# Two tiles side by side in 640 columns: theta and channel products of a linear-attention and mixing kernel

## The chip, the core and the metric

The kernel runs on one core of a Trainium2 chip. A core has five engines that work at the same time, each on its own list of instructions, in order: TensorE (PE: matrix products and transposes, results in PSUM), VectorE (DVE), ScalarE (ACT), GpSimd (POOL) and SyncE (SP, which here only issues transfers). They wait for each other by semaphores. Transfers between the main memory and the on-chip memory run on 16 DMA engines, which all issuing queues share. The metric is the device time of one execution in microseconds (us).

## The reference

Two stages follow each other. The first is a recurrent linear attention, for 4 batches and 8 heads of 40 columns over 768 steps, with one 40x40 state a head:

```
y_t   = r_t . state
Sa    = state . a_t
state = state * w_t - Sa x b_t + v_t x k_t
```

The heads side by side give x, of shape 4 x 768 x 320. The second stage mixes x:

```
theta = x @ w_theta                       (320 x 320)
y     = w_tok_r @ (x cos theta) + w_tok_i @ (x sin theta)   (768 x 768, over the steps of a batch)
u     = x + y
out   = u + max(u @ w_ch, 0)              (320 x 320)
```

## The kernel before, in words

The 768 steps of a batch are cut into 6 chunks of 128, so there are 24 tiles, numbered through the batches. Within a chunk the recurrence is turned into products of 128x128 blocks (scores with a triangular mask); from chunk to chunk of a batch only the state is handed on.

The order of all work is written out by hand in the text ORDER (line 19). An entry names a step, its tile, the engine that does it (A ScalarE, V VectorE, G GpSimd, S a DMA transpose from SP's queue) and, after the @, a PSUM bank: `EKBT:3A` is the copy of the transposed kb of tile 3 on ScalarE, `TRK:4@3` the transposition of kb of tile 4 into bank 3. A loop at the end of the kernel (line 800) issues the entries one by one, and each engine keeps that order. So an entry decides at once the engine's order, the PSUM bank and, for loads, the place in a DMA queue. PSUM has four single banks (sm0 to sm3) and two double ones (sc0, sc1). An entry that takes a bank again waits until its last reader is done.

The steps that matter below, with their lines:

- Loads: LDW, LDK, LDB, LDA, LDV, LDR (lines 301 to 331) bring w, k, b, a, v, r of a tile or of two, 160 or 320 KB each, from SP's queue; four of the first ones go from ScalarE's queue (`LDK:0A` and so on). LDC brings w_theta and w_ch, LDT 128 rows of a token weight; both are converted to 16 bits on the way and are issued by GpSimd (lines 721 and 740).
- The decays: LN, CSI, INVW, CSE, WI (lines 333 to 420). CSI and CSE are cumulative sums, made by products of 64 rows, two of them at a time in the two halves of TensorE's rows. CSE also makes the totals of a chunk, with products of 128 rows. Then KH (line 422) multiplies k and b by the inverse decays and AH (line 428) a by the decays.
- Transposes by TensorE (TRK, TRA, TRR, TRV, NUT, GD, XT, UT, WT) and their copies out of PSUM (EKBT, EAT, ERT, EVT, ENUT, EGD, EXT, EUT, EWT).
- Scores: PSI, PHI, LV, LU (line 534), eight products of 64 rows each, two side by side; EPSI, EPHI, ELV, ELU copy them out with the mask, on VectorE in one step, or on ScalarE with the mask made afterwards by GpSimd (MPSI, MPHI, MLV, MLU).
- The recurrence: X0, ENX, NU, ENU, GT, EGT, and the output of the attention: Y, EX (line 641), which writes x of the tile.
- The second stage: XT transposes x in three blocks of 128 columns (line 646), EXT copies them out, TH (line 664) multiplies the three with w_theta, ETH copies theta out, SIN makes cosine and sine, ZR multiplies them by x. YR (line 688) is one block of the token product: `YR:7.3` adds the block of chunk 3 of the batch to the rows of tile 7, so the last one of a tile needs z of the whole batch. EU makes u, UT and EUT transpose it, CH (line 707) multiplies with w_ch, EO makes the output, ST stores it.

x and u of a tile lie in 384 columns: 320 with data, 64 that are zero from the beginning. Columns 256 to 383 are the third block, and the third rows of w_theta and w_ch are 64 rows with data and 64 zero rows. So each theta and each channel product is three products of 128 rows and 320 columns.

Of the kernel before, what the change touches and what calls it, by code (L numbers as in the profile page):

```python
# [25 lines left out]
KH:3G LV:1@1 NU:1 EKBT:2A LU:0@0 ELV:1V LDW:4 TRA:2@0 ENU:1A LDV:3 ELU:0A NUT:1@3 AH:3G EAT:2V
GT:1@1 ENUT:1V PSI:2@1 TRK:3@0 EGD:0V EPSI:2V LDK:4 LDA:4 GI:1 EKBT:3A CV:2G TRA:3@3 LU:1@0
ELU:1A CR:2G PHI:2@1 EGT:1V X0:2@2 EAT:3V EPHI:2V MLU:0G ENX:2A LN:4A LDB:4 TRR:2@0 PSI:3@0
LDR:4 CV:3G PHI:3@1 MLU:1G Y:0@1 EPSI:3A MPSI:3G EPHI:3V NU:2 TRV:2@3 CSE:4@0 LDV:4 ENU:2A
ERT:2A EVT:2V GT:2@2 EX:0V WI:4A AH:4G CSI:4@1 INVW:4A Y:1@3 LDW:6 NUT:2@1 EGA:2V EGT:2V ERT:3A  # L30
ENUT:2V LV:2@0 LDA:5 TRV:3@2 EX:1V X0:3@1 ELV:2A KH:4G EVT:3V LU:2@1 ENX:3V ELU:2V LV:3@0
TRA:4@0 ELV:3A LDK:5 NU:3 TRK:4@3 LDB:5 GD:1@2 EAT:4V ENU:3A MLV:2G XT:0@0 EKBT:4V CR:4A GT:3@1
GI:3 EGD:1V EGT:3V PSI:4@1 EPSI:4V CV:4G PHI:4@0 LN:6A TRR:4@3 EPHI:4A NUT:3@2 MLV:3G Y:2@1
ENUT:3V LDB:6 LDA:6 AH:5G LDK:6 CSI:6@1 X0:4@2 EX:2V EXT:0A ERT:4A INVW:6A TRV:4@0 ENX:4V
MPHI:4G LDV:5 KH:5G LU:3@0 ERT:5A XT:1@1 NU:4 ELU:3V EXT:1A CSE:6@1 LDV:6 LDT:1.1G ENU:4A
TRA:5@3 WI:6A NUT:4@1 EVT:4V ENUT:4A TRK:5@2 LDK:7 EAT:5V AH:6G XT:2@0 EKBT:5V LV:4@0 TH:0@3
ELV:4V KH:6G PSI:5@1 GD:2@1 LDR:6 SIN:0A TH:1@2 LU:4@0 CV:5G GT:4@3 GI:4 EXT:2A EPSI:5V CV:6G
ZR:0G LDW:8 TRA:6@0 PHI:5@1 LDB:7 ELU:4A LDA:7 EGD:2V EGT:4V TH:2@1 SIN:1A EAT:6V MLU:4G SIN:2A
TRK:6@3 X0:5@0 GD:3@2 EPHI:5V EKBT:6V ENX:5A LDB:8 Y:3@1 ZR:1G EGD:3V EX:3V PSI:6@0 EPSI:6V
TRV:5@3 TRV:6@2 Y:4@1 LN:8A LDK:8 NU:5 PHI:6@1 EVT:6V ENU:5V EVT:5A CR:6G X0:6@2 EPHI:6V  # L40
LDT:1.0G KH:7G TRR:6@0 ENX:6A CSI:8@0 INVW:8A LDA:8 LDV:7 EX:4V NUT:5@3 LV:5@1 ELV:5A LDB:9
ERT:6V AH:7G ENUT:5V TRK:7@1 CSE:8@0 ERT:7V KH:8G TRA:7@3 WI:8A LDV:8 LV:6@1 EAT:7V EKBT:7V
ELV:6A LU:5@0 LDA:9 GD:4@0 NU:6 ELU:5V AH:8G PSI:7@1 TRK:8@3 LDK:9 ENU:6A EGD:4A CV:7A MLV:5G
PHI:7@0 EKBT:8A ZR:2G GT:6@1 NUT:6@2 EPSI:7V EPHI:7A EGT:6V TRV:7@0 TRA:8@3 ENUT:6V LDW:10
X0:7@1 EVT:7V LU:6@1 ENX:7V LV:7@0 LDR:8 ELU:6V Y:5@2 EX:5V EAT:8A XT:3@0 MPHI:7G AH:9G NU:7
EXT:3V XT:4@3 ELV:7A PSI:8@1 EXT:4A GD:6@2 KH:9G EPSI:8A EGD:6V TRA:9@0 LDV:9 PHI:8@0 TH:3@3
EPHI:8V ENU:7A XT:5@2 ETH:3A MLV:6G EAT:9V TRK:9@1 LN:10A LDA:10 LDK:10 NUT:7@3 EKBT:9V MPSI:8G
GT:7@0 GI:7 ENUT:7V PHI:9@1 EGT:7V LU:7@0 EXT:5V CV:8G TH:4@1 SIN:3A LDB:10 CR:8G LDB:11 TH:5@3
SIN:4A X0:8@0 LDK:11 EPHI:9V TRR:8@2 MLV:7G Y:6@1 ENX:8A ELU:7V LDW:12 CV:9A LDT:0.1G SIN:5A
EX:6V NU:8 ENU:8A ERT:8V LDT:2.1G LDV:10 ZR:5G CSE:10@1 WI:10A PSI:9@0 EPSI:9V Y:7@1 NUT:8@3  # L50
GT:8@0 GI:8 LDA:11 CSI:10@0 LDR:10 EX:7V WT:1.1@1 ENUT:8V INVW:10A EGT:8V EWT:1.1V TRV:8@3
ERT:9A LU:8@1 ELU:8V X0:9@0 EVT:8A WT:1.0@1 ENX:9A KH:10G TRV:9@2 LDV:11 LV:8@0 NU:9 EWT:1.0A
ELV:8V AH:10G WT:0.0@3 EWT:0.0V TRK:10@1 EVT:9A LV:9@1 ENU:9A EKBT:10A ELV:9V TRA:10@2 EAT:10A
LDK:12 WT:0.1@0 KH:11G ZR:3G WT:2.1@3 NUT:9@1 LN:12A ENUT:9V EWT:0.1V PHI:10@0 PSI:10@1 EPHI:10A
EPSI:10V LDT:2.0G TRK:11@2 GD:7@1 LDA:12 GT:9@0 EGD:7A CSE:12@0 CR:10G CV:10A EGA:9V EGT:9V
LU:9@1 EWT:2.1A LDB:12 Y:8@1 AH:11G EKBT:11V WI:12A MPHI:10G X0:10@0 LDW:14 ENX:10V TRR:10@3
TRV:10@2 ELU:9A LDV:12 CSI:12@0 INVW:12A ERT:10A LDC:0.2G EX:8V NU:10 YR:0.0@1 YR:0.1 LDK:13
ENU:10V EVT:10V ZR:4G YR:0.2 LDB:13 XT:6@0 EXT:6V YR:0.3 ERT:11A MLU:9G LV:10@1 WT:2.0@2 ELV:10A
YR:0.4 TRA:11@0 EWT:2.0V YR:0.5 EAT:11V AH:12G GD:8@3 GT:10@2 PHI:11@0 EGD:8A EU:0V EGA:10V
EPHI:11A CV:11G PSI:11@1 NUT:10@0 KH:12G LDR:12 EGT:10V EPSI:11V ENUT:10A TRV:11@1 TH:6@3 EXT:8S  # L60
Y:9@2 LDA:13 EVT:11A ETH:6A TRK:12@0 EX:9V LDT:5.1G LN:14A X0:11@1 MPHI:11G LDV:13 EKBT:12V
# [772 lines left out]
```

## Time and profile before

| what | before |
|---|---|
| median of 3 runs | 207.43 us (206.94 to 208.84) |
| the profiled execution, its own time | 206.92 us |
| its span, first to last instruction | 205.2 us |
| PE busy | 190.1 us, 93% |
| VectorE, ScalarE, GpSimd busy | 170.6, 154.3, 147.1 us |
| moved by DMA | 34.17 MB, mean 167 GB/s |

The profile is of one execution. Busy time is the time in which an engine has at least one instruction running; on PE, where products overlap, a busy engine isn't one at its peak, so the distance between starts is read as well. In the rows below a group stands as line, engine, operation, output<-inputs, form, count, and behind the bar its busy time, the mean ns of one and the idle time before it. A row of a timeline gives the start in us, the duration, engine, line, operation and count. A row of a table by stretch gives the stretch, its length, and for PE, PE's weight loads, VectorE, ScalarE and GpSimd the busy us and the count, then the granted clock (1.00 is full), the DMA share and GB/s.

### The profile page before, as it was taken

Reading aid. Unit: us, or ns where it says so; the run is one execution under the profiler, and the core shown is the slowest. Engines: PE = TensorE matmul, PEld = TensorE weight load, DVE = VectorE, ACT = ScalarE, POOL = GpSimd, SP = SyncE. Lnnn points to the kernel's source line nnn. Section 1 sums busy time; section 2 is a strip of 40 time slices with the busy share of each in tenths; the row PEclk is TensorE's granted clock in tenths of the full one; section 3 lists DMA queues with packets and bytes.
Section 4 is the critical chain, followed back from the end, with each engine's and each line's share of the span. In section 5 each row is a group of like instructions: output and inputs, shape, how many; then the busy total and the mean of one; then the engine's idle time right before and its main releaser. Section 6 shows DMA issues by size and latency. Waiting matters only on the chain.

```text
span 205.2 us, 7809 instructions
## 1 busy us (share of the span) xinstructions
PE 190.1 (93%) x3266; PEld 147.5 (72%) x3266; DVE 170.6 (83%) x334; ACT 154.3 (75%) x259; POOL 147.1 (72%) x157
## 2 busy tenths in 40 slices
PE   0389999999999999999999999999999999999992
PEld 0166777877777887887887877887877787777671
DVE  7256899999999997999799998989888797975653
ACT  2367799997989997999899788987898685822100
POOL 8225778899989699998966886993989785634000
PEclk9999999999999999999999999999999999999999
DMA  7999999998898999899489989987979996433342
GB/s 136 187 240 159 225 171 178 173 230 140 153 221 154 213 159 216 164 213 226 103 171 193 192 172 238 192 135 161 169 97 154 218 129 140 99 90 103 102 150 96
DMA packets 144802, 34.17 MB, mean 167 GB/s; under 512 B 139520, under 2 KB 144768, under 8 KB 144768
## 3 DMA queue, kind: packets, MB, share of 16 engines
q1 hardware_dynamic: 138176, 30.26, 76.5%
q0 software_dynamic: 2432, 2.77, 8.4%
q10 hardware_dynamic: 4160, 0.66, 2.2%
q8 instruction: 25, 0.41, 0.9%
q14 instruction: 9, 0.07, 0.1%
HBM read 29.13 MB, written 3.93 MB: 161 GB/s over the span
## 4 chain that ended last, share of the span: by engine, by line
PE 80%; ACT 6%; DVE 5%; issue 2%; ACTq 2%; POOL 2%; POOLq 0%; DVEq 0%
PE sm L278 39%; PE sc L278 22%; PE sm L282 20%; ACTq L331 1%; ACT kbT L270 1%; ACT psi L270 1%; DVE phi L275 1%; ACTq L326 1%; ACT Wi_two L412 1%; ACT lw_two L338 1%; POOL z L275 1%; DVE lamu L275 1%; DVE rvT L272 1%; POOL lamv L554 1%; POOL phi L554 1%
## 5 line engine op out<-in xcount | busy, mean ns | idle before, releaser
L275 POOL TENSOR_TENSOR kb<-raw_kb,invW_two 128x640 bf16<-128x640 f32 x22 | 33.9, 1542 | 5.5 <-ACT invW_two L373 3.6
L275 POOL TENSOR_TENSOR z<-cs,x 128x640 bf16<-128x640 f32 x22 | 30.8, 1403 | 5.3 <-ACT cs L677 5.3
L278 PE MATMUL sm<-z,wtok_r 128*128 128x320 bf16 x120 | 34.3, 299 | 0.0
L278 PE MATMUL sm<-z,wtok_i 128*128 128x320 bf16 x120 | 34.2, 299 | 0.0
L275 POOL TENSOR_TENSOR ah<-raw_a,Wi_two 128x320 bf16<-128x320 f32 x22 | 19.0, 866 | 8.5 <-issue 5.2
L275 DVE TENSOR_TENSOR psi<-sc,mask_p 128x1024 bf16<-128x1024 f32 x16 | 19.5, 1219 | 1.0 <-PE sc L278 0.9
L554 POOL TENSOR_SCALAR_AFFINE_SELECT psi<-psi 128x1024 bf16<-128x1024 bf16 x8 | 8.7, 1093 | 14.0 <-ACT psi L270 11.6
L275 DVE TENSOR_TENSOR phi<-sc,mask_p 128x1024 bf16<-128x1024 f32 x14 | 17.1, 1219 | 1.6 <-PE sc L278 1.4
L278 PE MATMUL sc<-aT,kbT 64*128 64x128 bf16 x384 | 17.3, 225 | 1.1 <-ACT kbT L270 0.7
L275 DVE TENSOR_TENSOR lamu<-sc,mask_p 128x1024 bf16<-128x1024 f32 x14 | 17.1, 1220 | 0.6 <-PE sc L278 0.3
L282 PE MATMUL sm<-ident,kb 128*128 128x128 bf16 x184 | 14.9, 227 | 2.6 <-DVE kb L275 2.3
L278 PEld LDWEIGHTS <-wtok_r 128*128 128x128 bf16 x144 | 14.0, 97 | 4.6 <-issue 0.3
L270 ACT COPY rvT<-sm 128x512 bf16<-128x512 bf16 x28 | 15.9, 593 | 1.3 <-PE sm L282 0.7
L278 PEld LDWEIGHTS <-wtok_i 128*128 128x128 bf16 x144 | 14.1, 98 | 3.9 <-issue 0.2
L275 DVE TENSOR_TENSOR lamv<-sc,mask_p 128x1024 bf16<-128x1024 f32 x13 | 15.9, 1220 | 1.0 <-PE sc L278 0.5
L677 ACT ACTIVATE cs<-sm 128x320 f32<-128x320 f32 x26 | 9.9, 452 | 8.5 <-PE sm L278 8.4
L278 PEld LDWEIGHTS <-kbT 64*128 64x128 bf16 x384 | 11.9, 97 | 5.8 <-issue 2.4
L278 PEld LDWEIGHTS <-rvT 64*128 64x128 bf16 (+1 forms) x272 | 13.6, 95 | 2.9 <-issue 0.5
L278 PE MATMUL sm<-kb,lamv 128*128 128x40 bf16 x192 | 15.0, 180 | 0.0
L278 PE MATMUL sm<-kb,lamu 128*128 128x40 bf16 x192 | 14.9, 179 | 0.0
L282 PEld LDWEIGHTS <-kb 128*128 128x128 bf16 x184 | 11.5, 101 | 4.2 <-DVE kb L275 2.3
L554 POOL TENSOR_SCALAR_AFFINE_SELECT lamu<-lamu 128x1024 bf16<-128x1024 bf16 x10 | 10.9, 1090 | 4.1 <-ACT lamu L270 4.1
(137 smaller groups left out, 625.0 us busy)
## 6 DMA issues: line engine op xcount, KB each, us to landing
raw_w_two<-in_w_dram SPq DMA_DIRECT2D x12, 320.0 KB, 4.8
...
```

The lines of the kernel that those rows point to most:

```text
L270: keep(nc.scalar.copy(out=out, in_=in_))
L272: keep(eng[e].tensor_copy(out=out, in_=in_))
L275: keep(eng[e].tensor_tensor(out=out, in0=in0, in1=in1, op=ALU.mult))
L278: keep(nc.tensor.matmul(out, lhsT=lhsT, rhs=rhs, start=start, stop=stop, skip_group_check=True))
L282: keep(nc.tensor.transpose(out=out, in_=in_, identity=ident))
L326: keep(queue[e].dma_start(out=tiles[i].raw_kb[:, j], in_=source(ap, i)))
L331: keep(queue[e].dma_start(out=t, in_=source(ap, i)))
L338: keep(nc.scalar.activation(out=q.lw[:, :, :, 0:D], in_=q.raw_w.rearrange("p h (j d) -> p j h d", j=2), func=AF.Ln))
L412: keep(nc.scalar.activation(out=two, in_=q.cse[:, LO:LO + 2 * DM + 16], func=AF.Exp))
L554: keep(nc.gpsimd.affine_select(out=flat, in_=flat, compare_op=ALU.is_ge, fill=0.0, base=-1, pattern=[[0, 2 * G], [1, 128]], channel_multip ...
L677: keep(nc.scalar.activation(out=cs[i % 5][:, c], in_=tiles[i].theta, func=AF.Sin, bias=(math.pi / 2, 0.0)[c]))
```

## The change

Three things change together.

First, x and u of two tiles that follow each other lie in 640 adjoining columns, for u in all pairs, for x in the pairs from (6, 7) on. These are five blocks of 128 columns: the even tile is transposed in two blocks (its columns 0 to 255), the odd one in three (columns 256 to 639 of the pair, of which the first block holds the last 64 columns of the even tile and the first 64 of the odd one). Theta and channel products of the even tile are two products of 128 rows, those of the odd tile also two, and the mixed block serves both: two products of 64 rows, one in the upper and one in the lower half of TensorE's rows, into two PSUM banks (new entries THR and CHR, which stand under the odd tile's number). So the even tile's result is complete only after THR or CHR. The weights are held in five blocks, and LDC has eight entries instead of four.

Second, the totals of CSE are an entry of their own, CST.

Third, the whole of ORDER is written anew. Among much else all loads of inputs come from SP's queue, the entries of ScalarE's queue are gone, and eight loads of weights (`LDT:1.0 LDC:0.1 LDC:0.3 LDC:0.2 LDC:0.4 LDT:1.1 LDC:0.0 LDT:0.0`) stand ahead of GpSimd's other work, where three (`LDC:0.0 LDT:0.0 LDC:0.1`) stood. theta is buffered for three tiles instead of four.

The begin of ORDER in both, and what stands around the last output:

```
-LDW:0 LDK:0A LDB:0 LDA:0A LDA:1 LDB:1A LDK:1 LDV:0A LN:0A LDC:0.0G LDT:0.0G CSI:0@0 LDC:0.1G CSE:0@1 WI:0A
-INVW:0A KH:0V TRK:0@0 AH:0V EKBT:0A TRA:0@3 LDW:2 EAT:0V LDR:0 KH:1V PHI:0@1 PSI:0@0
-EPSI:0A MPSI:0G CV:0A LDB:2 EPHI:0A AH:1V TRK:1@1 EKBT:1V LN:2A TRA:1@2 MPHI:0G LDV:1 TRV:0@3
...
+LDT:1.0G LDW:0 LDC:0.1G LDK:0 LDC:0.3G LDB:0 LDA:0 LN:0A CSI:0@0 LDW:2 LDC:0.2G LDC:0.4G LDV:0
+CSE:0@1 INVW:0A LDT:1.1G LDC:0.0G CST:0 WI:0A LDT:0.0G LDK:1 KH:0V TRK:0@0 EKBT:0A AH:0V TRA:0@3
+LDB:1 LN:2A LDA:1 EAT:0V CV:0A PSI:0@0 PHI:0@1 LDR:0 EPSI:0V X0:0@1 LDV:1 CSE:2@0 EPHI:0V KH:1V
...
-XT:7@2 EXT:7A LDB:14 LDT:3.1G ENX:11V TRA:12@3 LU:10@0 LV:11@1 ELU:10V NU:11 GD:9@0 EAT:12A
-MLV:10G YR:1.0@2 ELV:11A LDA:14 TH:7@3 ENU:11V PSI:12@0 ETH:7A EGD:9V PHI:12@1 LDT:3.0G EPSI:12V
...
+LDT:4.1G EXT:6V EAT:12V GT:10@3 GI:10 TH:6@0 ELV:11A EGT:10V MLU:10G THR:7@2 PSI:12@1 EPSI:12V
+X0:11@1 CV:12G TH:7 ETH:6A AH:13G ENX:11A GD:9@3 LDW:16 YR:1.0@0 EGD:9A PHI:12@0 ETH:7V LN:14A
...
-YR:23.3 YR:23.4 YR:23.5 EU:22V UT:22@1 CH:21@0 EU:23V EUT:22A EO:21V UT:23@3 CH:22@2 EUT:23V
-CH:23@1 EO:22V ST:21 EO:23V ST:22 ST:23
...
+YR:23.3 EU:21V UT:21@0 ST:19 YR:23.4 YR:23.5 EUT:21V CH:20@1 CHR:21@3 EU:23V UT:22@0 UT:23@2
+EO:20V CH:21 EUT:22A EUT:23V ST:20 EO:21V CH:22@1 ST:21 CHR:23@0 CH:23 EO:22V EO:23V ST:22 ST:23
```

The functions:

```
+    x_two = [consts.tile([128, 768 if 2 * n < lone else 2 * DM], BF16, name=f"x_two_{n}")
+             for n in range(NCH)]
...
+    def home(i, twins, one, two):
+        if i not in twins:
+            t = one[i % len(one)]
+            return t[:, 0:DM], t
+        t = two[i // 2 % len(two)]
+        if i % 2:
+            return t[:, DM:2 * DM], t[:, 256:2 * DM]
+        return t[:, 0:DM], t[:, 0:256]
...
     def tr_three(i, b, name, src):
         pt = bank(b, BF16)
         setattr(tiles[i], name, pt)
-        for kt in range(3):
+        for kt in range(src.shape[1] // 128):
             transpose(pt[:, kt * 128:kt * 128 + 128], src[:, kt * 128:kt * 128 + 128])
...
+    def mix(i, b, name, lhs, rhs, twins):
+        q = tiles[i]
+        if i not in twins:
+            setattr(q, name, bank(b))
+            for kt in range(3):
+                mm(getattr(q, name)[:, 0:DM], lhs[:, kt, :], rhs[:, kt, :], kt == 0, kt == 2)
+        elif i % 2 == 0:
+            setattr(q, name, bank(b))
+            for kt in range(2):
+                mm(getattr(q, name)[:, 0:DM], lhs[:, kt, :], rhs[:, kt, :], kt == 0, False)
+        else:
+            for kt in range(2):
+                mm(getattr(q, name)[:, 0:DM], lhs[:, 1 + kt, :], rhs[:, 3 + kt, :], False, kt == 1)
+
+    def mix_ends(i, b, name, lhs, rhs):
+        setattr(tiles[i], name, bank(b))
+        for c in range(2):
+            mm(getattr(tiles[i - 1 + c], name)[:, 0:DM], lhs[rows(c), 0, :], rhs[rows(c), 2, :],
+               c == 1, c == 0)
...
     def weight_load(n):
-        dst, src = ((wth, moe_w_theta), (wch, moe_w_ch))[n // 2]
-        if n % 2 == 0:
-            keep(nc.gpsimd.dma_start(out=dst[:, 0:2, :], in_=src[0:256, :].rearrange(
-                "(a p) d -> p a d", p=128)))
+        dst, src = ((wth, moe_w_theta), (wch, moe_w_ch))[n // 4]
+        first, part = n % 2, n % 4 // 2
+        if part == 0:
+            keep(nc.gpsimd.dma_start(
+                out=dst[:, 3 * first:3 * first + 2, :],
+                in_=src[64 * first:64 * first + 256, :].rearrange("(a p) d -> p a d", p=128)))
         else:
-            keep(nc.gpsimd.dma_start(out=dst[0:64, 2, :], in_=src[256:320, :]))
+            keep(nc.gpsimd.dma_start(out=dst[rows(first), 2, :],
+                                     in_=src[256 * (1 - first):256 * (1 - first) + 64, :]))
```

More of the change, by code (lines that the diff above doesn't have):

```diff
@@ L26 @@
[L26 to L61, printed above, removed]
@@ new lines @@
+EXT:9S PSI:13@1 EX:11V EPSI:13A MPSI:13G EWT:3.1V CSE:14@0 CST:14 GT:12@0 EUT:0S WT:3.0@1
+EVT:13V UT:1@2 NUT:12@3 EGT:12V LN:16A WI:14A EUT:1V TRK:14@0 ENUT:12V EWT:3.0V LDT:5.1G
+WT:4.1@2 EKBT:14A AH:14G EWT:4.1V LDV:14 LU:12@1 ELU:12V LV:13@0 LDR:14 YR:3.0@3 ELV:13A AH:15G
+X0:13@1 LDK:15 YR:3.1 TRA:14@2 ENX:13A EAT:14V YR:3.2 YR:3.3 LDV:16 CH:0@0 CHR:1@2 MPHI:13G
+PHI:14@0 CV:14A EO:0V ST:0 PSI:14@1 CH:1 ZR:6G EPHI:14V NU:13 Y:12@0 ENU:13A YR:3.4 EPSI:14A
+EO:1V LDV:15 TH:8@1 YR:3.5 EX:12V MPSI:14G CR:14A THR:9@2 TH:9 ETH:9A EU:3V WT:5.1@0 TRV:14@3
@@ new lines @@
+ZR:10G ST:3 EKBT:17A TRA:17@0 LDW:20 EGA:15V YR:6.3 LV:16@1 ELV:16A CSE:18@0 EGT:15V MPHI:16G
+CST:18 WI:18A EAT:17V LDA:18 UT:5@2 X0:16@3 EUT:5V CH:4@0 ENX:16V CHR:5@2 EO:4V CSI:18@1 CV:17A
+PSI:17@0 NU:16 INVW:18A KH:18G CH:5 ST:4 YR:6.4 YR:6.5 EPSI:17V ENU:16A LDV:18 TRV:17@0 EVT:17A
+GD:14@3 EU:6V PHI:17@1 EGD:14V EO:5V NUT:16@1 LDB:19 XT:12@3 GT:16@0 ENUT:16V LDK:19 EPHI:17A
+EXT:12A EGA:16V EGT:16V Y:15@2 TRK:18@1 ST:5 TH:12@3 EXT:14S MPHI:17G EKBT:18V LV:17@0 THR:13@0
+AH:18G LU:16@1 EX:15V X0:17@1 ELU:16V CR:18G TH:13 TRA:18@2 LDW:22 SIN:12A ENX:17A YR:7.0@3
```

249 lines of the change are left out of this document (140 added, 109 removed).

## The prediction

> **What bounds the kernel now.** I read the page first, for the shares, then the table by stretch, for where each engine is full.
>
> ```profile
> span 205.2 us, 7809 instructions
> PE 190.1 (93%) x3266; PEld 147.5 (72%) x3266; DVE 170.6 (83%) x334; ACT 154.3 (75%) x259; POOL 147.1 (72%) x157
> PE 80%; ACT 6%; DVE 5%; issue 2%; ACTq 2%; POOL 2%; POOLq 0%; DVEq 0%
> ...
> 30.00:60.00 30.00, 29.39 (x613) 23.08 (x609) 28.71 (x51) 27.26 (x46) 27.75 (x28) 1.00 0.97 181
> 60.00:190.00 130.00, 129.51 (x2267) 101.94 (x2261) 114.41 (x200) 107.66 (x186) 103.14 (x102) 1.00 0.87 164
> 190.00:205.20 15.20, 11.54 (x89) 7.65 (x86) 7.78 (x17) 1.14 (x3) 0.00 (x0) 0.99 0.37 117
> ```
>
> The second number of a stretch is its length, then come PE, PE's weight loads, VectorE, ScalarE and GpSimd. From 60 to 190 us PE is busy 129.51 of 130 us, VectorE 114.41 (88%). Busy is not work, since matmuls overlap, so I look at starts: whether one matmul begins as soon as the one before allows.
>
> ```profile
> 102.13 0.30 PE L278 MATMUL sm<-z,wtok_i 128*128 128x320 bf16 x1
> 102.27 0.30 PE L278 MATMUL sm<-z,wtok_r 128*128 128x320 bf16 x1
> 102.40 0.30 PE L278 MATMUL sm<-z,wtok_i 128*128 128x320 bf16 x1
> 102.54 0.33 PE L282 MATMUL sm<-ident,x 128*128 128x128 bf16 x3
> 102.80 0.62 PE L278 MATMUL sc<-aT,kbT 64*128 64x128 bf16 x16
> 103.36 0.34 PE L282 MATMUL sm<-ident,nu 128*128 128x128 bf16 x3
> ```
>
> A 320-column product holds PE for 0.135 us (102.13, 102.27, 102.40). Three transposes take 0.26 us when 64-row products follow (102.54 to 102.80). There is no stall here beyond that, and the chain that ended last is 80% PE. So a microsecond of PE work removed after 60 us is a microsecond of time, if the new list keeps PE as full. Before 60 us the four engines are all at 91 to 98%, and before that the loads count.
>
> **The change part by part.**
>
> *Products of theta and channel (THR, CHR).*
>
> ```profile
> L278 PE MATMUL sm<-wch,uT 128*128 128x320 bf16 x72 | 13.7, 300 | 0.1
> L278 PE MATMUL sm<-wth,xT 128*128 128x320 bf16 x72 | 13.2, 299 | 0.0
> L282 PE MATMUL sm<-ident,x 128*128 128x128 bf16 x57 | 6.3, 220 | 0.1
> L282 PE MATMUL sm<-ident,u 128*128 128x128 bf16 x42 | 4.6, 219 | 0.1
> ```
>
> Three products a tile, 72 for theta and 72 for the channels; the third is half zeros. Nine pairs of x tiles (6 to 23) and all twelve pairs of u tiles go from six full products to four full and two of 64 rows. That takes away 42 x 0.135 = 5.7 us. What a pair of 64-row products costs shows where the kernel already makes such pairs, in the cumulative sums: four of 64x320, two and two side by side.
>
> ```profile
> 37.66 0.18 PE L278 MATMUL sm<-kb,lamv 128*128 128x40 bf16 x1
> 37.68 0.18 PE L278 MATMUL sm<-kb,lamu 128*128 128x40 bf16 x1
> 37.79 0.45 PE L278 MATMUL sc<-lw_two,pair_inc 64*128 64x320 bf16 x4
> 38.17 0.21 PE L278 MATMUL sm<-gt,aT 128*128 128x80 bf16 x1
> ```
>
> Four take 0.38 us to the next start (37.79 to 38.17). One after another they would need 4 x 0.135 = 0.54, so they do run side by side: two steps of 0.135 are 0.27, and 0.11 us is left, the price of going back to 128 rows. The way in costs about 0.09: a 128x40 product has 0.02 to the next (37.66 to 37.68), ahead of the 64-row ones 0.11 (37.68 to 37.79); likewise 0.26 against 3 x 0.056 for the transposes above. A visit to 64 rows thus costs 0.19 us beside its work. So: added 21 pairs x 0.135 = 2.8 us, net -2.8 us, plus or minus the visits.
>
> That last part could undo the change: 21 lonely pairs would cost 21 x 0.19 = 4.0 us. I counted the visits in both lists, taking neighbouring score, sum and pair products as one: 84 before, 81 after, because the totals of the cumulative sum became a step of their own (CST) and 13 of the 21 pairs stand beside other 64-row products (PSI, PHI, LV, LU, CSI or another pair). So -3 x 0.19 = -0.6 us. The Trainium skill, "TensorEngine Tiling (Array Packing)", Key Properties, says that changing the tiling mode drains TensorE; the trace agrees, with 0.09 us in and 0.11 us out. By that rule with no regard to neighbours this part would come out at +1.2 us instead of -3.4.
>
> *Transposes.* The even tile of a pair is transposed in two blocks instead of three, and more go by the DMA transpose. On PE the x transposes fall from 57 to 39, the u ones from 42 to 29; six more for the token weights and four each of NUT and TRV come in, four of GD go: net -21 x 0.056 = -1.2 us, all after 60 us but a few. DMA transposes rise from 28 to 34 on SP's queue. They stand behind other entries of that queue, and every load behind them waits; I take 0, between 0 and 6 x 1.2 us of SP (an x transpose holds SP 1.2 us by its row), which costs only where a load is late.
>
> ```profile
> L448 SPq DMA_TRANSPOSE xT<-x x5: 1184/1207/1672, 82.0 to 185.4; - x5
> ```
>
> *PE in all:* -2.8 - 0.6 - 1.2 = -4.6 us.
>
> *The other engines.* The new list moves work between them.
>
> ```profile
> L275 DVE TENSOR_TENSOR lamu<-sc,mask_p 128x1024 bf16<-128x1024 f32 x14 | 17.1, 1220 | 0.6 <-PE sc L278 0.3
> L272 DVE COPY rvT<-sm 128x512 bf16<-128x512 bf16 x18 | 8.8, 491 | 0.8 <-PE sm L282 0.7
> L523 DVE TENSOR_SCALAR nx<-sm 128x320 bf16<-128x320 f32 x13 | 6.4, 489 | 2.3 <-PE sm L278 2.0
> L272 DVE COPY kbT<-sm 128x1024 bf16<-128x1024 bf16 x16 | 11.0, 686 | 2.3 <-PE sm L282 2.2
> ```
>
> VectorE: two more masked scores (+2.4), eight more r and v copies (+3.9), eleven fewer nx and nu (-5.4), three fewer kbT (-2.1), and a net of six more small copies of about 0.42 (+2.5): +1.3 us on 170.6. ScalarE loses some 4 us, GpSimd is unchanged. Until tile 18 VectorE does about 6 us more than before and after that as much less. It has 12% to spare after 60 us, so I take 0, and keep +3 us as the far end, half of that bulge.
>
> *The start.* Two things oppose each other. For: the inverse weights (INVW) come ahead of WI, and the first scores are masked on VectorE in one step.
>
> ```profile
> 7.83 0.72 ACT L412 ACTIVATE Wi_two<-sc 128x656 f32<-128x656 f32 x1 [1.68 <-PE sc L278]
> 9.17 0.83 DVE L275 TENSOR_TENSOR kb<-raw_kb,invW_two 128x640 bf16<-128x640 f32 x1 [3.76 <-ACT invW_two L373]
> 14.36 1.08 POOL L554 TENSOR_SCALAR_AFFINE_SELECT psi<-psi 128x1024 bf16<-128x1024 bf16 x1 [8.13 <-ACT psi L270]
> 17.78 1.54 POOL L275 TENSOR_TENSOR kb<-raw_kb,invW_two 128x640 bf16<-128x640 f32 x1 [1.07 <-ACT invW_two L373]
> 22.45 1.54 POOL L275 TENSOR_TENSOR kb<-raw_kb,invW_two 128x640 bf16<-128x640 f32 x1
> ```
>
> That saves the 0.72 of Wi ahead of the first kb, about 0.5 of products, and the 1.08 of the GpSimd mask: 2.3 to 3.5 us on tile 0. Against: eight loads stand at the head of GpSimd's queue instead of three (192, 160, 40, 40, 160, 192, 160 and 192 KB, 1136 KB instead of 392), and the four early loads of ScalarE's queue (q10) move to SP's (q1). The three windows' DMA rows:
>
> ```profile
> q1 hardware_dynamic: 2525, 0.40, 73.6%
> q10 hardware_dynamic: 2357, 0.37, 70.9%
> ...
> q0 software_dynamic: 469, 0.39, 80.6%
> q1 hardware_dynamic: 704, 0.13, 32.2%
> q10 hardware_dynamic: 407, 0.07, 17.0%
> ```
>
> From 4 to 8 us (first two rows: packets, MB, share) the input loads move 0.77 MB, 0.19 a us. From 8 to 11 us GpSimd's 0.39 MB are moved and the inputs get 0.20 MB, 0.07 a us. With 1136 KB that stretch lasts 3 x 1136/392 = 8.7 us, and 5.7 us more at 0.07 instead of 0.19 is 0.7 MB, or 3.6 us of loading; if q10's turns fall away too, 0.04 a us, it is (0.19 - 0.04) x 8.7 less (0.19 - 0.07) x 3, 0.9 MB or 4.9 us. It strikes k and b of tiles 1 to 3: their kb steps, at 17.78 and 22.45 before, come some 4 us later, and tile 1 waits for data that tile 0's earlier finish can't use. By 30 us both stand near the first x tile, VectorE some 1.3 us behind. The Trainium skill, "DMA: Bandwidth & Descriptors", Queues, rings and completion order, has each DMA engine take turns between queues packet by packet; the fall from 0.19 to 0.07 agrees, and by it the inputs lose one of their two turns here. I take +2 us for the start; from -2 (only the gain counts) to +5 (all the delay).
>
> *The end.* The last row product starts at 199.35, the last output step at 201.69.
>
> ```profile
> 199.35 0.30 PE L278 MATMUL sm<-z,wtok_i 128*128 128x320 bf16 x1
> 201.69 0.49 DVE L715 SCALAR_TENSOR_TENSOR oo<-sm,u 128x320 f32<-128x320 f32 x1
> ```
>
> In the new list the outputs of 22 and 23 both wait for the last pair, so one 0.49 us step comes after instead of between; and theta of 22 is closed only with x of 23, so z of 23 follows later than the 2.7 us of PE work in the list covers: I take +0.7, between 0 and 1.5.
>
> *The sum.* -4.6 + 2 + 0.7 = -1.9 us. The profiled execution took 206.92 us (205.2 span and 1.7 around it): 205.0. It lies at the low end of the runs shown (median 207.43, 206.94 to 208.84), so for a median I add 0.2: **205.2 us**, 1.1% under the median. The bounds of the terms: -4.6 - 2 = -6.6 at best, and -4.6 + 5 + 1.5 + 3 = +4.9 at worst.
>
> **The rivals.**
>
> - *PE's saving comes through whole and the start gains* (no loss by the loads, since before 60 us something else binds): -4.6 - 0.5 to -1, 201.5 to 202.5. For it: tile 4 needs its k only late; the DMA waits in the trace of before are few. Against: by the turns above tile 1 must wait.
> - *The loads bind the start* (turns taken by GpSimd's eight loads): +4.9 instead of +2, and VectorE's bulge behind it, +1 to +3: 206.9 - 4.6 + 4.9 + 0.7 + 1 is 208.9, with +3 it is 210.9; half of it within 1%. It decides if kb of tile 2 starts after 23 us.
> - *Slower: the closing product waits.* A pair's even half can't be read before the odd tile's transposed copy lies in SBUF, the pair stands in PE's queue, and all behind it stands too; two banks are held meanwhile, of four. Price: the wait, 21 times. A copy of 0.35 to 0.5 us and its two hand-overs against the PE work that the list puts between (for 11, 3 and 5 it is 0.8 to 1.1 us, for 23 0.8) leaves little. From 0.1 us a pair the gain of 1.9 is gone; at 0.25 us a pair it is +5.3 - 1.9, 210.5 us. Against: the trace of before shows no waits of PE for copies after 60 us.
> - *The pairs don't run side by side* (banks or rows conflict): +21 x 0.135 = +2.8, 208 us. Against: the four 64x320 products in 0.38 us.
>
> **How the numbers follow.** Forecast 0.50 (203 to 207.4; two thirds of it over 1% faster), whole saving 0.13, loads 0.20, closing product 0.13, not side by side 0.04. The likeliest case's own range is 203 to 207.4. The range of all is 201.5 to 210.2: below it lies a little of the whole saving, above it the closing product's upper part and a third of the loads, together under 0.2. About 1%, 2 us, is what a measurement of this kernel tells from no change. Faster by over 1%: 0.33 + 0.13 = 0.46. Slower by over 1% (over 209.5): the closing product 0.13 and half of the loads 0.10, 0.23. The rest, 0.31, within 1%.
>
> **What would show it.** In the profile after: 64x320 products of wch and wth, 24 and 18 of them, two by two starting together; about 0.135 us to the next 64-row start; PE's rows 21 fewer; between 60 us and the end no PE wait over 0.3 us for xT or uT copies. For the start: q0's stretch from 8 us to 16 or 17, kb of tile 1 after 16 us and of tile 2 near 22. If kb of tile 2 stands at 18, the start term is wrong; if PE's waits behind 60 us sum to over 3 us, the sum is wrong at the premise that PE stays full.

## The result, and the profile after

| | before | after |
|---|---|---|
| median of 4 runs | 208.13 us (206.94 to 210.64) | 214.89 us (213.04 to 215.20) |
| ratio after to before | | 1.0329, 95% interval 1.0280 to 1.0378 |
| span of the profiled execution | 205.2 us | 213.5 us |

The changed kernel is 3.3% slower; 205.2 us and a range up to 210.2 us were forecast. Medians here are over all executions; the ratios leave out those that took over 1.5% longer than the kernel's fastest (two of four in e8 and e18 below, one of four in e4 and e12), so a ratio can differ from the quotient of two medians.

The page of the changed kernel, same parts as shown of before (span, busy time, the chain that ended last):

```profile
span 213.5 us, 7781 instructions
PE 189.1 (89%) x3245; PEld 143.5 (67%) x3245; DVE 172.3 (81%) x327; ACT 152.3 (71%) x252; POOL 147.6 (69%) x158
PE 45%; DMA 19%; DVE 11%; ACT 8%; POOL 8%; SPq 4%; issue 3%; DVEq 0%; POOLq 0%; ACTq 0%
```

PE's rows are 21 fewer, as foretold, but its share of the chain fell from 80 to 45%, and DMA, which was not in it, has 19%. The table by stretch of the changed kernel (columns as before: stretch, length, PE, its weight loads, VectorE, ScalarE, GpSimd, clock, DMA share, GB/s):

```profile
30.00:60.00 30.00, 28.48 (x589) 22.54 (x587) 27.87 (x48) 28.50 (x48) 25.73 (x26) 1.00 0.99 183
60.00:190.00 130.00, 126.22 (x2264) 97.72 (x2263) 114.02 (x201) 104.72 (x173) 103.39 (x103) 1.00 0.90 162
190.00:213.50 23.50, 17.60 (x144) 10.50 (x141) 11.50 (x24) 3.88 (x11) 3.67 (x3) 0.98 0.34 104
```

From 60 to 190 us PE is busy 126.22 us where it was 129.51, for almost the same number of instructions (2264, 2267). What it stood for is in the view of waits. Behind 60 us the kernel before has one row, the changed one ten (who waited, for whom: us in total, times, longest):

```profile
PE sm L282 <- ACT nu L521: 0.2, 1, 0.2
```

```profile
PE sm L296 <- DMA uT<-u_two: 1.2, 2, 0.7
PE sm L300 <- DMA wtok_row<-in_moe_w_tok_i_dram: 0.7, 1, 0.7
PE sm L296 <- POOL psi L575: 0.6, 1, 0.6
PE sm L300 <- POOL ah L293: 0.6, 2, 0.4
PE sc L296 <- DVE u_two L742: 0.6, 1, 0.6
PE sm L296 <- ACT nu L542: 0.6, 1, 0.6
PE sm L300 <- DVE rvT L290: 0.4, 1, 0.4
PE sm L300 <- ACT rvT L288: 0.4, 1, 0.4
PE sm L296 <- DMA xT<-x_two: 0.4, 1, 0.4
PE sc L296 <- DVE kbT L290: 0.2, 1, 0.2
```

They sum to 5.7 us, for DMA, VectorE, ScalarE and GpSimd in turn, none of them the one new bound. The prediction named a sum over 3 us as the sign that its premise is wrong, and any wait over 0.3 us for xT or uT as a sign against it: here they come to 0.7.

The view leaves out short waits. So I also measured from the starts of PE's instructions: for each two that follow each other, by group and form, the distance's lower quartile over all traces of this study is taken as work, and what a distance has beyond it (over 0.04 us) as standing. By stretch, in us; "first" is PE's first product, "last" the time from PE's last start to the end:

| kernel | first | work | standing | 0-60 | 60-160 | 160-end | last |
|---|---|---|---|---|---|---|---|
| before | 6.2 | 165.6 | 29.5 | 15.6 | 11.2 | 2.8 | 3.8 |
| after | 4.9 | 161.2 | 43.4 | 20.8 | 14.7 | 7.9 | 4.0 |

Work fell by 4.4 us (4.6 were priced), the first product comes 1.3 earlier, the last part is 0.2 longer, and PE stands 13.9 us more: +8.4 in all, against 8.3 between the spans. So the question of the experiments is where 13.9 us of standing come from. The 29.5 us of before hold the start and the short hand-overs that any list has. The measure is an estimate: other ways to pool the neighbours move all rows alike by up to 3 us, and against each other by about 1 us, e4 below by 2 and e7 by 4; the difference between before and after stays within 0.3.

### The profile page after: what moved, and what is told of

Read it like the earlier page. It is cut to its first block, busy times and chain, and to the rows that moved or that the text cites. A ratio compares the mean times of both kernels' runs of the same rounds, so it can differ in the third digit from the quotient of the medians.

```text
span 213.5 us, 7781 instructions
## 1 busy us (share of the span) xinstructions
PE 189.1 (89%) x3245; PEld 143.5 (67%) x3245; DVE 172.3 (81%) x327; ACT 152.3 (71%) x252; POOL 147.6 (69%) x158
## 4 chain that ended last, share of the span: by engine, by line
PE 45%; DMA 19%; DVE 11%; ACT 8%; POOL 8%; SPq 4%; issue 3%; DVEq 0%; POOLq 0%; ACTq 0%
PE sm L296 21%; PE sc L296 12%; PE sm L300 12%; DMA raw_kb<-in_b_dram 7%; DMA wtok_row<-in_moe_w_tok_i_dram 3%; DMA raw_v<-in_v_dram 3%; DMA raw_a<-in_a_dram 2%; POOL kb L293 2%; DVE rvT L290 2%; DMA uT<-u_two 2%; DVE lamu L293 2%; POOL ah L293 2%; ACT rvT L288 1%; POOL z L293 1%; ACT kbT L288 1%
## 5 line engine op out<-in xcount | busy, mean ns | idle before, releaser
L293 POOL TENSOR_TENSOR kb<-raw_kb,invW_two 128x640 bf16<-128x640 f32 x22 | 33.9, 1540 | 23.7 <-ACT rvT L288 13.5
L293 POOL TENSOR_TENSOR z<-cs,x_two 128x640 bf16<-128x640 f32 x22 | 30.7, 1402 | 4.5 <-ACT cs L714 4.5
L293 DVE TENSOR_TENSOR lamu<-sc,mask_p 128x1024 bf16<-128x1024 f32 x21 | 25.6, 1217 | 1.7 <-PE sc L296 1.7
L296 PE MATMUL sc<-aT,kbT 64*128 64x128 bf16 x384 | 18.3, 225 | 1.9 <-ACT kbT L288 0.7
L300 PE MATMUL sm<-ident,kb 128*128 128x128 bf16 x184 | 14.9, 228 | 5.6 <-DVE kb L293 4.9
L293 DVE TENSOR_TENSOR psi<-sc,mask_p 128x1024 bf16<-128x1024 f32 x14 | 17.1, 1220 | 3.0 <-PE sc L296 2.9
L288 ACT CAST lamv<-sc 128x1024 bf16<-128x1024 f32 x14 | 14.2, 1014 | 4.4 <-PE sc L296 4.4
L751 DVE SCALAR_TENSOR_TENSOR oo<-sm,u_two 128x320 f32<-128x320 f32 x24 | 11.6, 488 | 6.9 <-PE sm L296 6.8
L296 PEld LDWEIGHTS <-kbT 64*128 64x128 bf16 x384 | 12.5, 98 | 6.4 <-issue 2.3
L575 POOL TENSOR_SCALAR_AFFINE_SELECT psi<-psi 128x1024 bf16<-128x1024 bf16 x10 | 10.9, 1092 | 8.3 <-ACT psi L288 6.7
L290 DVE COPY rvT<-sm 128x512 bf16<-128x512 bf16 x26 | 14.3, 560 | 2.0 <-PE sm L300 1.1
L575 POOL TENSOR_SCALAR_AFFINE_SELECT lamv<-lamv 128x1024 bf16<-128x1024 bf16 x14 | 15.3, 1093 | 0.8 <-ACT lamv L288 0.8
L296 PE MATMUL sm<-kb,lamu 128*128 128x40 bf16 x192 | 14.9, 180 | 0.0
```

Of the source, the lines that this page charges most:

```text
L288: keep(nc.scalar.copy(out=out, in_=in_))
L290: keep(eng[e].tensor_copy(out=out, in_=in_))
L293: keep(eng[e].tensor_tensor(out=out, in0=in0, in1=in1, op=ALU.mult))
L296: keep(nc.tensor.matmul(out, lhsT=lhsT, rhs=rhs, start=start, stop=stop, skip_group_check=True))
L300: keep(nc.tensor.transpose(out=out, in_=in_, identity=ident))
L575: keep(nc.gpsimd.affine_select(out=flat, in_=flat, compare_op=ALU.is_ge, fill=0.0, base=-1, pattern=[[0, 2 * G], [1, 128]], channel_multip ...
```

## The experiments

All runs of three rounds; the ratio is to the kernel before on the same chip. Standing is by the same measure as above, in brackets where the profiled execution is one that the ratio leaves out, so that it reads too high. It also holds what PE loses where its clock is lowered (see e12).

| run | median us | ratio (95% interval) | PE work | standing | 0-60, 60-160, 160-end |
|---|---|---|---|---|---|
| after | 214.89 | 1.0329 (1.0280 to 1.0378) | 161.2 | 43.4 | 20.8, 14.7, 7.9 |
| e1 late weights | 212.58 | 1.0204 (1.0135 to 1.0274) | 161.3 | 40.2 | 19.0, 14.9, 6.4 |
| e2 before, eight loads | 210.46 | 1.0105 (1.0045 to 1.0165) | 165.4 | 33.9 | 18.3, 11.6, 3.9 |
| e3 unpaired | 213.71 | 1.0283 (1.0205 to 1.0361) | 162.7 | 39.6 | 20.7, 13.1, 5.8 |
| e4 tail on PE | 216.05 | 1.0366 (1.0280 to 1.0453) | 162.0 | 43.4 | 21.5, 14.2, 7.7 |
| e5 old start | 216.70 | 1.0466 (1.0402 to 1.0531) | 162.0 | 43.1 | 17.5, 18.4, 7.2 |
| e6 old start, unpaired | 217.50 | 1.0518 (1.0444 to 1.0592) | 164.5 | 41.3 | 16.5, 17.8, 7.0 |
| e7 pairs in old list | 237.35 | 1.1454 (1.1379 to 1.1529) | 165.8 | 61.1 | 17.8, 26.6, 16.7 |
| e8 late, unpaired | 212.12 | 1.0144 (1.0084 to 1.0204) | (162.8) | (40.3) | (18.1, 15.7, 6.5) |
| e9 loads ahead | 213.36 | 1.0306 (1.0225 to 1.0388) | 161.0 | 41.6 | 18.8, 18.3, 4.5 |
| e10 mid transposes on PE | 216.76 | 1.0506 (1.0421 to 1.0591) | 163.3 | 42.9 | 17.9, 18.0, 7.0 |
| e11 a on ScalarE's queue | 220.38 | 1.0619 (1.0501 to 1.0737) | 161.5 | 48.2 | 20.7, 21.0, 6.4 |
| e12 before, more DMA transposes | 225.42 | 1.0881 (1.0781 to 1.0982) | (165.0) | (50.4) | (15.8, 23.9, 10.7) |
| e13 new then old | 209.84 | 1.0109 (1.0070 to 1.0148) | 164.1 | 35.5 | 18.5, 13.6, 3.4 |
| e14 old then new | 214.11 | 1.0319 (1.0259 to 1.0380) | 164.6 | 36.8 | 16.5, 14.1, 6.1 |
| e15 new then old, late | 213.50 | 1.0274 (1.0221 to 1.0328) | 163.4 | 41.5 | 17.9, 19.7, 4.0 |
| e16 old then new, late | 220.17 | 1.0606 (1.0556 to 1.0656) | 165.1 | 44.2 | 16.9, 20.1, 7.2 |
| e17 three parts | 213.36 | 1.0302 (1.0273 to 1.0332) | 165.7 | 35.6 | 16.8, 14.5, 4.4 |
| e18 old start, paired, loads mended | 213.11 | 1.0205 (1.0129 to 1.0282) | (163.0) | (38.9) | (16.7, 15.6, 6.6) |

### The start: the early loads (e1, e2)

e1 delays four of the changed kernel's eight first loads:

```
-LDT:1.0G LDW:0 ... LDC:0.2G LDC:0.4G ... LDT:1.1G LDC:0.0G ... LDT:0.0G
+LDW:0 ... LDC:0.2G ... LDC:0.0G ... AH:4G LDT:0.0G ... AH:5G LDT:1.1G ... AH:6G LDT:1.0G ... LDC:0.4G LDC:0.5G
```

> The changed kernel with four of its eight early weight loads (three of a token weight, one of w_ch, 736 KB of 1136) moved to between 35 and 90 us. Theory (start): the eight loads take the DMA engines from the inputs of tiles 1 to 3, and the delay lasts to the end since every engine is full afterwards: kb of tile 1 back from 16.9 us to 12 or 13, of tile 2 from 22.8 to 18 or 19, and the time 4 to 5 us shorter, 210 to 211 us beside 214.9. Rival (later): the start's delay is taken up by slack behind it and the time is lost in waits after 50 us: kb comes earlier likewise, but the time falls by less than 1.5 us.

e2 gives the kernel before as many early loads:

```
-... LDC:0.1G ...
+... LDC:0.1G LDT:1.1G LDT:1.0G LDC:0.2G LDC:0.3G LDT:2.1G ...
```

> The kernel before, with five more weight loads at the head of GpSimd's queue (three of token weights, two of w_ch, so 1168 KB there instead of 392). Theory (start): inputs of tiles 1 to 3 come some 4 us later, and so does the end: 3 to 4.5 us longer than before. Rival (later): less than 1.5 us longer.

Delaying the four loads gains 1.25 points of ratio, 2.6 us; adding them to before costs 2.2 us (0.9 to 3.4). The rows of the changed kernel say how: from 7 to 15.5 us GpSimd's queue moves 1.16 MB and the inputs 0.51 (packets, MB, share of 16 engines), 0.06 MB a us.

```profile
q0 software_dynamic: 1402, 1.16, 83.5%
q1 hardware_dynamic: 3046, 0.51, 42.2%
```

In the chain of work of the changed kernel (start, us, what), b of tile 1 lands after 10.23 us; in e1 the same load takes 6.20:

```profile
6.62 10.23 DMA raw_kb<-in_b_dram
16.94 0.83 DVE kb L293
...
22.80 1.54 POOL kb L293
```

```profile
6.75 6.20 DMA raw_kb<-in_b_dram
```

So the loads cost about 2.4 us in time. But e1 was to come to 210 or 211, and its 212.58 is still 2% slower than before: the larger part lies elsewhere.

### The pairs (e3, e7, e8)

e3 is the changed kernel's list with whole products (THR and CHR taken out, three products a tile, u in five buffers):

```
-TH:6@0 ... THR:7@2 ... TH:7
+TH:6@0 ... TH:7@2
```

> The changed kernel in its own order but without pairs: every theta and channel product three full products again, THR and CHR gone, transposes of three blocks, u in five buffers. PE's work rises by 21 x 0.135 us of products and 7 x 0.056 us of transposes and falls by 7 visits to 64 rows of 0.19 us: +1.9 us. Theory (PE's saving is real): about 2 us longer than the changed kernel, 216 to 218 us. Rival (the closing product waits): the even tiles no longer wait for the odd ones, so it is as fast or faster, 212 to 215 us.

PE's work rises by 1.5 us and its standing falls by 3.8, of which 2.1 behind 160 us; the time is the same within the intervals, rather shorter. The 3.8 us read too high for the pairs: the profiled executions are the longest of the changed kernel and the shortest of e3, 2.2 us apart, where the medians are 1.2 apart. The waits for DMA uT, 1.2 us with pairs, are 0.2 without, those for the token row and for ScalarE's nu are gone (waits of PE behind 60 us in e3):

```profile
PE sc L290 <- DVE u L736: 0.6, 1, 0.6
...
PE sm L290 <- DMA uT<-u: 0.2, 1, 0.2
PE sc L290 <- DVE kbT L284: 0.2, 1, 0.2
PE sm L294 <- POOL ah L287: 0.2, 1, 0.2
```

e7 puts all 21 pairs into the list before. What follows an even tile's product (its copy, its output step) moves behind the pair with it, the totals CST are their own entry and LDC has eight; the rest keeps its order:

```
-TH:6@3 ... TH:7@3
+(at the odd tile's place) TH:6@a THR:7@b TH:7      likewise CH, CHR
```

> The list before with all 21 pairs, nothing else reordered: the even tile's product is moved to the odd one's place (with what follows it), the rows of the weights that the pairs need are loaded in two more loads behind 45 us. The list has 100 visits to 64-row mode instead of 84, since most pairs stand alone there. By the profile's prices: 21 pairs instead of 42 tail products -2.8, transposes -1.2, 16 visits at 0.19 +3.0, in sum -1.0: 207.2 us if nothing waits. If the closing pair waits for the odd tile's copy, and other work behind it in TensorE's order with it: over 209 us.

Not 1 us faster but 30 us slower. PE's work, 165.8 against 165.6, has changed little (the estimate is good to 4 us here); its busy time from 60 to 190 us fell from 129.51 to 112.86 (table by stretch of e7), and the waits of e7 behind 60 us are of another kind:

```profile
60.00:190.00 130.00, 112.86 (x1922) 83.94 (x1918) 96.86 (x166) 96.16 (x161) 92.75 (x95) 0.97 0.80 148
```

```profile
PE sm L298 <- DVE oo L749: 3.7, 7, 1.0
PE sm L298 <- ACT cs L712: 3.4, 4, 1.7
PE sc L294 <- ACT rvT L286: 2.2, 1, 2.2
PE sm L298 <- ACT kbT L286: 2.1, 1, 2.1
PE sm L294 <- ACT rvT L286: 1.3, 1, 1.3
PE sm L298 <- ACT th L286: 1.0, 2, 0.5
```

The closing product's own input is little of it: a row not shown has 0.6 us, in two waits, for the copy uT. The largest rows are oo and cs, with th 8.1 us: steps that read the results of pairs out of their banks, before the transposes (L298) that come next can have a bank. A pair holds two of the four single banks and hands both to the readers at one time, and this fits. But 8.1 us are not 30. The other rows wait for copies of operands, and three stretches of 3.4 us at half the granted clock (see e12) cost up to 5 us more in the profiled execution; what put those copies late was not followed up. So pairs put into a list as it stands lose far more than they save.

e8 takes both away, pairs and early loads. It leaves the new order and what came with it: inputs from SP's queue alone, eight loads of w_theta and w_ch, three buffers of theta:

> The changed kernel with the late start loads of the first experiment and without the pairs: the new order alone. Additive by the two single runs (-2.3 and -1.2): 211.4 us, which leaves 3.2 us to the new order itself against 208.2 before, although its list has 10 visits to 64-row mode fewer (1.9 us). If the two hide each other: 212.5 us.

Its ratio lies within 1.0084 to 1.0204, that of e1 (with pairs) within 1.0135 to 1.0274. Twice, then, taking the pairs out has changed nothing that these runs can tell. What is left, 1.4% or 3.0 us by the ratio and 2.1% by the medians of all (212.12, before 207.77), is the new order's with what came with it, although its PE work is 2.8 us less than before: transposes fewer, and its list has 74 visits to 64-row mode instead of 84.

### SP's queue and the DMA transposes (e4, e9 to e12)

The chain has 19% DMA, so I suspected SP's queue, on which loads stand behind waiting DMA transposes. e4 makes five late DMA transposes on PE; e9 moves the loads ahead; e10 makes twelve DMA transposes of the middle on PE; e11 lets ScalarE issue the loads of a; e12 gives the kernel before eight of the DMA transposes that the changed one has and it has not.

```
e4:  -EUT:14S EUT:15S EUT:16S EUT:17S EXT:22S   +UT:14@2 EUT:14A ... XT:22@1 EXT:22A
e9:  every LDK, LDB, LDA, LDV, LDR, LDW 30 entries earlier, or right behind what frees its buffer
e10: -EXT:8S ... EUT:11S                        +XT:8@0 EXT:8A ... UT:11@3 EUT:11V
e11: -LDA:6 ... LDA:23                          +LDA:6A ... LDA:23A
e12: -XT:9@0 EXT:9V ... UT:4@3 EUT:4A           +EXT:9S ... EUT:4S
```

> The changed kernel with the last DMA transposes (u of 14 to 17, x of 22) made by TensorE and copied by ScalarE, which is idle for two thirds of that time. In the trace PE stands 0.9, 0.5 and 0.6 us for those transposes between 192 and 198 us; the five transposes add 0.7 us to PE. Theory (late transposes at the end): 1.5 to 2 us shorter, near 213 us. Rival (another step is late in their place): within 0.5 us of 214.9.

> The changed kernel with the late start loads (212.6 us), and behind tile 2 every input load that SP issues stands 30 entries earlier in the list, or right behind the step that frees its buffer (21 entries earlier on average), so ahead of the waiting DMA transposes of x and u. Theory S (SP's queue is the bound of the new order: it issues for 192 us of the changed kernel's span against 174 of before, and loads stand behind DMA transposes that wait): the waits for raw inputs vanish from the chain that ended last and the time falls by 2 us or more, to 210.5. Theory N (the loads only show in the chain since their engines were late anyway): within 0.8 us of 212.6.

> The changed kernel with the late start loads, and the 12 DMA transposes of x 8, 9, 10, 13, 14, 16 and u 0, 2, 4, 9, 10, 11 made by TensorE and a copy on ScalarE or VectorE at the same places of the list. TensorE gets about 28 transposes at 0.056 us, 1.6 us, VectorE and ScalarE six copies each of 0.4 to 0.5 us; SP loses 12 issues of 1.2 us and their waits, some 25 us. Theory S: 2 to 4 us faster than 212.6 although TensorE has more work. Theory N: 1.6 us slower or more, 214 to 215.

> The changed kernel with the late start loads, and the loads of a from tile 6 on issued by ScalarE's queue, which takes 18 issues of about 0.9 us off SP (16 us). Theory S: 1 to 3 us faster than 212.6, less what ScalarE loses by issuing. Theory N: 0 to 1.5 us slower, since ScalarE is put behind by 18 issues.

> The kernel before with eight more DMA transposes in place of TensorE's (x 9, 10, 13, 14, 16, u 0, 2, 4), which the changed kernel also makes on SP's queue; else its own list. TensorE loses 24 transposes of 0.056 us (1.3 us), ScalarE and VectorE eight copies. Theory S: SP's 174 us of issuing become 184 and loads behind the transposes come late, 2 to 4 us slower than before (210 to 212). Theory N: the same or up to 1.3 us faster (207 to 208).

Four times SP was relieved or its loads were brought forward, and no time fell. In e9 PE stands for the DMA transpose of u, now behind the loads (first row, waits of PE from 100 us). e10 spares SP twelve issues and is 3 points of ratio slower than e1. So theory S, that SP's queue as such bounds the new order, finds no support, and relief by these ways does not pay. It is not ruled out cleanly, since each run brought a cost of its own: e9 that wait, e10 2.0 us more PE work than e1 and twelve copies, e11 one wait of 5.5 us for ScalarE's inverse weights.

```profile
PE sm L292 <- DMA uT<-u_two: 3.9, 2, 3.5
```

But e12 shows what a DMA transpose costs in a list not made for it. PE's work was to fall, and the time rose by 8.8%, beyond either expectation (waits of PE in e12 behind 60 us):

```profile
PE sm L273 <- DMA uT<-u: 9.0, 2, 5.1
PE sm L273 <- DMA xT<-x: 4.0, 3, 3.0
```

The transposed copy comes late, and PE's queue stands in order behind its product. These rows are 13.0 us. A second cost follows them: from within such waits, or shortly behind, the granted clock reads 0.5 for a while, and PE counts as busy all the same. It is seen best in e16 (below), behind a wait of 6.7 us that ends at 149.1 us; first the stretch behind it, then the one after (table by stretch):

```profile
150.00:154.00 4.00, 4.00 (x43) 3.21 (x41) 1.15 (x3) 2.18 (x4) 2.40 (x3) 0.50 0.00 0
155.00:159.00 4.00, 3.96 (x82) 3.30 (x80) 3.42 (x5) 2.15 (x5) 3.41 (x3) 1.00 0.58 127
```

In 4 us of a busy PE there are 43 products instead of 82. In e12 three such stretches, of 3.4, 6.8 and 6.8 us by the trace, come with waits of 3.9, 5.1 and 3.0 us; where PE works in them it loses half, an estimated 6.7 us. With the 13.0 that is 19.7, near the 20.0 us between the spans. e5, e6, e7, e9, e11, e15 and e16 have such stretches too, of 3.4 to 10.2 us in all, behind waits of 1.7 to 6.7 us. The kernel before, the changed one, e1 to e4, e8, e10, e13, e14, e17 and e18 have none until the very end, so that the clock has no part in the 3.3%. Not every wait brings it: the changed kernel stands 4.1 us from 13.7 us on at full clock.

An exchange in one place of such a list, either way (e10, e12), costs more than its instructions.

### Joining the two lists (e5, e6, e13 to e18)

The unpaired lists have the same steps, so a first part of the one can be followed by what is left in the order of the other. "New" is with the late loads.

```
e5, e6:   before up to Y:6, then new (e5 with pairs, e6 without)
e13, e14: cut behind ENU:15 (some 120 us): new then before; before then new; no pairs
e15, e16: the same, cut behind ENU:18
e17:      before up to Y:6 (three LDT earlier, as in e18), new up to ENU:15, before; no pairs
e18:      e5 with LDT:0.1 LDT:2.1 LDT:2.0 some 90 entries earlier
```

> The changed kernel with the first part of its list put back: every step up to y_out of tile 6 stands as in the list before (start loads, x of tiles 0 to 5, their evictions), all that is left follows in the new order, with all 21 pairs. In the changed kernel x of tile 3 comes at 53.9 us instead of 47.1 (6.8 us late), and the end 8.3 us late. Theory A (the loss sits in the first tiles of the new list, behind the early loads and VectorE's queue): tile 3 at 47 again and the end 6 to 7 us earlier than the changed kernel, 208 to 209 us. Theory B (the new order loses by waits spread over the whole run, some of them the pairs'): the rest of the list falls behind again, 211 us or more.

> The run above without the pairs: each product whole in its own three, u in five buffers. Theory 'the pairs' waits eat what they save' (unpairing the changed kernel took 1.2 us off): 1 to 1.5 us under the run above, 207 us if theory A holds there. Theory 'pairs pay where the list ahead of them is not late': 2 us above the run above, 210 to 211.

> No pairs, late start loads. The new list up to the eviction of nu of tile 15 (about 120 us), then all that is left in the order of the list before. The whole new list without pairs and early loads took 212.1 us, the whole old one 207 to 208. Theory 'the loss is in the first half': 212. Theory 'the loss is in the end, where TensorE waits for DMA transposes and u': 208. Theory 'spread over both': 210.

> The reverse: the old list up to the eviction of nu of tile 15, then all that is left in the new order; no pairs. First half: 207 to 208. End: 212. Spread: 210. If the two halves do not add up with the run above to 212.1 + 207.5, the cut itself costs.

> As the first of these, cut at the eviction of nu of tile 18 (about 140 us): only the last 60 us in the old order. If the loss sits in the end: 208 to 209 as with the earlier cut. If between tiles 15 and 18: 212 here and less there. If in the first half: 212.

> The reverse of that: old order up to the eviction of nu of tile 18, then the new order. End: 211 to 212. First half or tiles 15 to 18: 207 to 208.

> No pairs. The old list up to y of tile 6 with the token-weight loads 2.0, 2.1 and 0.1 some 90 entries earlier, then the new list up to the eviction of nu of tile 15, then the old one. The run with new, then old order took 209.8 us, and TensorE stands 3 us more in its first 60 us than in the list before. If start, middle and end are separate losses and the seams cost nothing: 207 us, no slower than before. If each seam costs about 2 us (the two complementary joins at tile 15 sum to 4.4 us more than the two whole lists): 209 to 210.

> The earlier run with the old start and the whole new rest with pairs (216.7 us), in which TensorE stood 3.5 us for a token-weight row at 72 us, now with the three token-weight loads some 90 entries earlier. If that late load was what made it slow: 212 to 213. If the seam costs by other waits: 215 or more.

e5 missed both theories upward, by a wait of its own (waits of PE in e5 up to 100 us): the cut brought three loads of token weights behind each other, and PE stood for the last.

```profile
PE sm L297 <- DMA wtok_row<-in_moe_w_tok_i_dram: 3.3, 1, 3.3
```

e18 mends only that and takes off 2.6 points of ratio, 5.4 us: the wait of 3.3, and an estimated 2.2 for the half clock behind it, which e18 doesn't have. Its ratio then equals that of e1 (1.0205, 1.0204), its median over all executions is rather higher. So no gain of the old start over the new one with late loads is seen, what the cut costs included. e5 and e6, with and without pairs, differ by less than their intervals; but they have 10.2 and 3.4 us at half clock, so this pair says little about the pairs.

Of all lists with a part of the new order, e13 has the least loss, 1.1%. With the old order in the end PE stands 3.4 us behind 160 us, and its waits from 100 us on are two; with the new end, in e14, it stands 6.1 us there, 3.3 more than before, and the waits for DMA transposes and for u are among the rows (waits of PE from 100 us on, first e13, then the first four of e14):

```profile
PE sm L292 <- ACT nu L538: 0.5, 1, 0.5
PE sc L292 <- ACT lamv L284: 0.4, 1, 0.4
```

```profile
PE sm L296 <- ACT v L284: 1.7, 1, 1.7
PE sm L292 <- DMA uT<-u: 0.7, 1, 0.7
PE sc L292 <- DVE u L738: 0.6, 1, 0.6
PE sm L292 <- DMA xT<-x_two: 0.3, 1, 0.3
```

But the sums do not close: e13 and e14 together have 2.8 points more than a whole new list without pairs and a whole old one (1.09 + 3.19 against 1.44), e15 and e16 have 7.4 points more. Each cut makes a wait of its own: 1.7 us for v in e14, and in e16, where standing from 60 to 160 us is 20.1 us, one for lamv, with the half clock behind it that is shown above:

```profile
PE sc L292 <- ACT lamv L284: 6.7, 1, 6.7
PE sc L292 <- ACT psi L284: 1.2, 1, 1.2
```

e17, to join the best parts, has two cuts and 3.0%. No version beats the kernel before. That the new end stands some 3 us more is seen where e14 is set beside e13 and before; where the rest of the order's loss sits, the joins can't settle.

## Why the prediction was wrong

*Products and transposes: right.* -4.6 us of PE work was priced, 4.4 are gone. The 64-row products run two at a time, 24 and 18 of them (groups of the changed kernel). By PE's starts the two of a pair begin 2 to 4 ns apart, and where more 64-row work stands behind them it begins 0.135 to 0.148 us later, as for one product:

```profile
L296 PE MATMUL sm<-wch,uT 128*128 128x320 bf16 x48 | 10.5, 301 | 1.2 <-DMA uT<-u_two 1.2
L296 PE MATMUL sm<-wch,uT 64*128 64x320 bf16 x24 | 3.7, 305 | 0.0
L296 PE MATMUL sm<-wth,xT 64*128 64x320 bf16 x18 | 2.8, 302 | 0.0
```

The price of a visit to 64-row mode held too. In e7, where most pairs stand alone, a pair starts 0.23 us behind a 320-column product instead of 0.135, and the next full product 0.24 us behind the pair instead of 0.135 to 0.148: about 0.19 in all, more than the 0.135 that a pair saves, so lonely pairs are worth nothing even where nothing waits. The Trainium skill, "TensorEngine Tiling (Array Packing)", Key Properties, has a change of mode drain TensorE; this trace agrees, with some 0.1 us on each way. The rival "not side by side" is out.

*The start: right in mechanism, too small in sum.* The loads' delay was priced at 3.6 to 4.9 us; delaying four of them gives back 2.6, and five more cost the kernel before 2.2. kb of tile 1 came at 16.94 (after 16 foretold), of tile 2 at 22.80 (near 22). But the +2 that was taken is this delay less a gain of 2.3 to 3.5 us on tile 0, and that gain doesn't last. kb of tile 0 does start at 6.4 us instead of 9.2, yet up to 60 us PE stands 5.2 us more, 3.9 with its earlier first product taken off, and x of tile 3 comes at 53.9 us instead of 47.1. Even with the late loads of e1 PE stands 3.4 us more there. So by this measure the term was some 4, within its range of -2 to +5 and twice what went into the sum.

*DMA transposes: cost taken as nothing, wrong.* "I take 0": PE waits 1.6 us for the DMA transposes uT and xT in the changed kernel. The bound was put as SP's time, 1.2 us an issue; what counts is how late the copy comes to PE's in-order queue, up to 5.1 us in e12.

*The end: right for what it priced, but the waits ahead of it had no term.* +0.7 (to 1.5) was taken for what comes behind the last row product; that stretch is 6.4 us instead of 5.8. But PE stands 5.1 us more behind 160 us than before, nearly all of it ahead of that product. Unpairing takes up to 2.1 of that away, the old order of the end (e13, 3.4, against e14, 6.1) 2.7.

*VectorE: not shown to bind.* It is busy 1.7 us more than before (1.3 foretold; ScalarE 2.0 less, 4 foretold). PE waits for VectorE 1.2 us behind 60 us, by the three rows of u_two, rvT and kbT. No run changed its load alone.

*The step that failed* is the premise of the whole sum: "a microsecond of PE work removed after 60 us is a microsecond of time, if the new list keeps PE as full." It doesn't. PE's waits behind 60 us went from 0.2 to 5.7 us; its standing grew by 8.6 us there, twice the saving of 4.4, and by 13.9 us in all. The rows of before showed how full PE is in the list before, and I carried that over to another list. By the ratios the loss of 3.3% divides into 1.25 points for the early loads, 1.4 for the new order with what came with it (2.1 by the medians), and about 0.6 that is within the intervals; the pairs bring no change that these runs can tell. That the early loads cost is shown from both sides; that the order loses is shown by what is left without pairs and early loads, not by naming its waits.

*The rival "the closing product waits"* had a price for just this: from 0.1 us a pair the gain is gone, at 0.25 it would be 210.5. Unpaired, PE stands up to 3.8 us less, 0.18 us a pair, and works 1.5 us more: about what the pairs save they lose, as that rival says. But the rows name DMA transposes for it, and in e7 banks, more than the odd tile's copy; and the rival explains why the pairs' saving doesn't show, not why the kernel is slower. The rival "loads bind" counted 4.9 us for the loads, and 2.2 to 2.6 were found. The first rival's 201.5 to 202.5 is 201.5 to 202.0 by its own terms.

What stays open: which entries of the new order make PE stand longer from 60 to 160 us (13.1 in e3 and 14.9 in e1 against 11.2). Relief of SP's queue in four ways did not help; the loads of VectorE and ScalarE were not varied alone.
